# A convolution and a gated unit on one core: row exchanges by transfers in both halves, four more spectrum buffers, closing sums on VectorE, and a rewritten order

## The chip, the core and the metric

The kernel runs on one core of a Trainium2 chip. A core has TensorE (PE in the profile; its weight loads are PEld), VectorE (DVE), ScalarE (ACT), GpSimd (POOL) and SyncE (SP, which here does nothing but issue transfers, one after another). The time is the device time of the program in microseconds (us). The number to be changed is the median of three runs.

## The reference

With `xn` the layer norm of `u` (2048 tokens, 512 channels), the output is the sum of three things:

```python
x = A_u
xn = _layernorm(x, axis=-1)
return x + _A_ref(xn, ...) + _B_ref(xn, B_w_gate, B_w_up, B_w_down)

# _A_ref: a state space convolution, by FFT of length 2L, plus a skip
K = jnp.einsum("dn,dnl,dn->dl", Cc, P, dB).real      # kernel of each channel, P = exp(dt*A*l)
y = irfft(rfft(u) * rfft(K))[:, :L] + u * Dskip

# _B_ref: a gated linear unit, 512 -> 1792 -> 512
h = _sigmoid(x @ w_gate) * (x @ w_up)
return h @ w_down
```

## The kernel before

The gated unit is dense work for TensorE: four groups of 512 tokens (`grp`, L1016), in each 14 blocks of `w_gate` products (L1036) and 14 of `w_up` products (L1060), four matmuls of 512 columns to a block, then four `w_down` products (L1105) of 14 matmuls each. ScalarE takes the sigmoid (L1048), and ScalarE or VectorE takes `up` out of PSUM and multiplies (L1072, L1076).

The convolution is laid between this work. It has these stages:

- The kernel spectra: for four chunks of channels, tables are made on VectorE and ScalarE (L735 to L795) and multiplied on TensorE (L820); each chunk's result goes out to `k_scr` (L831) and comes back (L836). The products of the fourth chunk free the memory of the tables.
- The first transform of `xn`: L694, out to `z_scr` by way of a copy (L287 is the line of the helper that all such copies share).
- Sixteen units (L867 to L935): two halves of the channels (`p` 0 and 1), in each eight groups of frequencies in the order of `UNITS`. A unit loads its part of `z_scr` (L874), makes the spectrum of x on TensorE (L882), copies it to a buffer `xx` (`ex`, L886), exchanges rows between pairs of 32 partitions within `xx`, loads a table `E` (L897), makes the kernel spectrum (L904), multiplies both on VectorE (L909 and L913), turns the product back on TensorE (`mv_`, L926), copies it (`ev`, L930) and stores it to `v_scr` (L933).
- The reload of `v_scr` (`reload`, L963): three parts, the first half's units (part 0), and of the second half the first six units (part 1) and the last two (part 2); each in four pieces. Two of the pieces of part 2 are issued on ScalarE's queue, the others on SyncE's.
- The last transform (L985, L988), added to the unit's output. For token tiles of the first three groups it is `final` (L990): the sum with the gated unit's output, which lies in `glu_sb`. For tiles in `FIN_ACT` (1, 3 and 5 of six) TensorE adds that output by two matmuls with the identity (`fi`, L999) and ScalarE copies the sum (L1007); for the others VectorE adds while it reads PSUM (L1011). The last group's four tiles are summed in L1125. The `w_down` products of the last group are laid between.

The exchange of rows is done in two ways. In the first half (`p == 0`, L890) each unit issues four transfers of 64 KB from SBUF to SBUF on SyncE's queue. In the second half (L893 to L896) VectorE does four copies of 32 partitions.

What sets the order: nothing is scheduled at run time. Every step is an entry of a list (`_Plan.add`, L264), numbered in the order in which the code makes them, and `ORDER` (L202) is a permutation of these numbers written out by hand. Each engine, and each queue of transfers, works its steps strictly in the order in which they stand there; what a step needs of others it waits for with semaphores, and everything behind it on that engine or queue waits too. Buffers that rotate are pools (`_Slot`): `acq` takes the home that has been free longest, `rel` gives it back. The spectrum buffers `xx` have three homes (L856), and a fourth once the tables are free (L846). The buffers of outputs (`ot`) are three.

Of the kernel before, what the change touches and what calls it, by code (L numbers as in the profile page):

```python
# [44 lines left out]
FIN_ACT = (1, 3, 5,)  # L45
# [18 lines left out]
KB = 1024  # L64
# [114 lines left out]
def _consts():  # L179
# [138 lines left out]
def kernel(  # L318
# [74 lines left out]
    OFF = {}  # L393
# [10 lines left out]
    xn = at(OFF["xn"], [NT, D])  # L404
# [457 lines left out]
    def slot(pool, shape):  # L862
        sl = _Slot(pool)
        return sl, lambda: at(HOME[pool][sl.idx], shape)

    v_st = [[] for _ in VPART]
    for p in range(NP):  # L867
        dsl = slice(DW * p, DW * p + DW)
        for u in UNITS[p]:
# [22 lines left out]
            else:  # L892
                def f_sw(xx=xx):  # L893
                    for b in range(4):
                        V.tensor_copy(out=half_of(xx, b, 1), in_=half_of(xx, b ^ 1, 0))  # L895
# [299 lines left out]
```

## Time and profile before

| | |
|---|---|
| runs, median (lowest, highest) | 219.86 us (218.53, 219.88) |
| profiled execution, span on the core | 217.6 us |
| PE busy | 209.0 us, 96% |
| DVE busy | 193.8 us, 89% |
| ACT busy | 179.5 us, 83% |
| DMA, packets of the main queue | 63.8% of 16 engines |

The profile is one execution; its span runs from the first instruction to the last on the core, and it carries no other time of its own. The runs' median lies 2.26 us above that span. Durations and moments in this document that have no other source are those of the profiled execution, counted from the start of its span. Matmuls are pipelined: a row gives 380 ns for one of 512 columns, while a block of four takes 0.86 us.

### The profile page before, as it was taken

How to read it: one execution, taken by the hardware profiler on the slowest of the kernel's cores; microseconds unless marked ns; L12 is line 12 of the kernel's file. 1: busy time of each engine (PE TensorE's matmuls, PEld its weight loads, DVE VectorE, ACT ScalarE, POOL GpSimd, SP SyncE). 2: the span in 40 equal slices, each digit the busy share in tenths (PEclk: the TensorE clock that was granted, in tenths of full speed). 3: DMA queues.
4: the chain of work that ended last, by engine and by line, in shares of the span. 5: the costliest groups of instructions: out<-in, count | busy, mean ns of one | idle time of the engine just before them, and what ended most of it. 6: DMA issues, size and time to landing. Idle time of an engine off the chain costs nothing.

```text
span 217.6 us, 4946 instructions
## 1 busy us (share of the span) xinstructions
PE 209.0 (96%) x1876; PEld 104.0 (48%) x1876; DVE 193.8 (89%) x438; ACT 179.5 (83%) x286; POOL 18.8 (9%) x40
## 2 busy tenths in 40 slices
PE   7979999999999999989999999999999999999894
PEld 2435444444444454435455565445546556544463
DVE  3989999999999999999999999999999999970433
ACT  3799999999999999869989999976897999960111
POOL 1410202002100020012000002010800000000000
PEclk9999999999999999999999999999999999999999
DMA  6999936001463689865697679929959969984974
GB/s 186 316 369 390 299 116 146 0 3 48 145 156 97 233 249 156 264 143 105 166 271 202 183 224 209 239 79 216 216 116 252 282 188 263 267 245 139 269 256 166
DMA packets 51530, 42.80 MB, mean 197 GB/s; under 512 B 16434, under 2 KB 43571, under 8 KB 51507
## 3 DMA queue, kind: packets, MB, share of 16 engines
q1 hardware_dynamic: 50338, 40.60, 63.8%
q0 software_dynamic: 864, 1.57, 5.5%
q10 hardware_dynamic: 304, 0.33, 0.6%
q8 instruction: 14, 0.23, 0.4%
q14 instruction: 10, 0.07, 0.1%
HBM read 25.97 MB, written 12.85 MB: 178 GB/s over the span
## 4 chain that ended last, share of the span: by engine, by line
PE 64%; DMA 17%; ACT 8%; SPq 7%; issue 2%; DVE 0%; ACTq 0%
PE bank L1060 18%; PE bank L1036 16%; PE bank L1105 10%; PE pair L904 7%; SPq L421 7%; DMA wu_sb<-in_B_w_up_dram 5%; PE pair L926 4%; ACT big L287 4%; DMA z_scr<-big 3%; DMA big<-big 3%; DMA big<-z_scr 2%; DMA v_scr<-big 2%; PE pair L882 2%; PE pair L820 2%; ACT us_sb L1072 2%
## 5 line engine op out<-in xcount | busy, mean ns | idle before, releaser
L287 ACT ACTIVATE big<-pair 128x1024 bf16<-128x1024 f32 x64 | 66.2, 1060 | 4.9 <-PE pair L926 1.5
L1060 PE MATMUL bank<-xnT,wu_sb 128*128 128x512 bf16 x224 | 54.5, 380 | 0.5 <-DMA wu_sb<-in_B_w_up_dram 0.4
L1036 PE MATMUL bank<-xnT,wg_sb 128*128 128x512 bf16 (+1 forms) x220 | 50.7, 368 | 1.9 <-DMA wg_sb<-in_B_w_gate_dram 1.8
L1105 PE MATMUL bank<-wd_sb,hT_sb 128*128 128x512 bf16 (+1 forms) x238 | 50.4, 367 | 0.0
L1036 PEld LDWEIGHTS <-wg_sb 128*128 128x128 bf16 x236 | 22.2, 98 | 26.9 <-issue 2.5
L1105 PEld LDWEIGHTS <-hT_sb 128*128 128x128 bf16 x238 | 22.6, 98 | 25.2 <-issue 1.9
L1060 PEld LDWEIGHTS <-wu_sb 128*128 128x128 bf16 x224 | 20.6, 98 | 25.2 <-issue 3.0
L1048 ACT ACTIVATE hT_sb<-bank 128x512 bf16<-128x512 f32 x52 | 30.9, 636 | 1.2 <-PE bank L1036 1.1
L735 DVE TENSOR_TENSOR big<-big 128x1024 bf16<-128x1024 bf16 (+4 forms) x40 | 26.8, 670 | 0.3 <-ACT big L287 0.2
L736 DVE TENSOR_TENSOR big<-big 128x1024 bf16<-128x1024 bf16 (+4 forms) x40 | 26.7, 667 | 0.0
L1072 ACT ACTIVATE us_sb<-bank 128x512 bf16<-128x512 f32 x40 | 25.9, 648 | 0.3
L909 DVE TENSOR_TENSOR big<-big 128x2048 bf16<-128x2048 bf16 x16 | 19.5, 1218 | 0.6 <-PE pair L926 0.3
L904 PE MATMUL pair<-big 128*128 128x256 bf16 x160 | 19.8, 273 | 0.0
L789 ACT ACTIVATE sq_sb<-big 128x256 bf16<-128x256 bf16 (+2 forms) x20 | 13.8, 691 | 5.1 <-DVE big L741 4.9
L904 PEld LDWEIGHTS <-big 128*128 128x128 bf16 x160 | 15.4, 98 | 4.9 <-issue 1.0
L1076 DVE TENSOR_TENSOR hT_sb<-hT_sb,us_sb 128x512 bf16<-128x512 bf16 x40 | 16.5, 418 | 0.4 <-ACT us_sb L1072 0.3
L740 DVE TENSOR_TENSOR big<-big 128x512 bf16<-128x512 bf16 (+4 forms) x40 | 16.5, 414 | 0.1
L741 DVE TENSOR_TENSOR big<-big 128x512 bf16<-128x512 bf16 (+4 forms) x40 | 16.5, 413 | 0.0
L1007 ACT ACTIVATE big<-pair 128x1024 bf16<-128x1024 f32 x3 | 3.1, 1023 | 15.2 <-PE pair L985 12.4
L895 DVE COPY big<-big 32x1024 bf16<-32x1024 bf16 x32 | 13.4, 419 | 0.6
L1011 DVE TENSOR_TENSOR big<-pair,glu_sb 128x1024 bf16<-128x1024 f32 x2 | 2.5, 1226 | 11.7 <-PE pair L985 8.1
L541 DVE BATCH_NORM_STATS2 stats<-big 128x6 f32<-128x512 bf16 x15 | 9.8, 682 | 3.4 <-DMA big<-in_A_u_dram 3.4
(104 smaller groups left out, 244.3 us busy)
## 6 DMA issues: line engine op xcount, KB each, us to landing
big<-c_E SPq DMA_DIRECT2D x16, 320.0 KB, 3.9
z_scr<-big SPq DMA_DIRECT2D x16, 256.0 KB, 2.9
big<-z_scr SPq DMA_DIRECT2D x16, 256.0 KB, 4.9
v_scr<-big SPq DMA_DIRECT2D x16, 256.0 KB, 3.1
big<-in_A_u_dram SPq DMA_DIRECT2D x4, 512.0 KB, 8.2
big<-big SPq DMA_DIRECT2D x32, 64.0 KB, 3.6
wu_sb<-in_B_w_up_dram SPq DMA_DIRECT2D x2, 896.0 KB, 10.7
wd_sb<-in_B_w_down_dram SPq DMA_DIRECT2D x1, 1792.0 KB, 15.1
```

What stands on the lines that cost most here:

```text
L287: nc.scalar.activation(out=get(out), in_=get(in_), func=ACT.Identity)
L735: V.tensor_tensor(out=wide(outp), in0=wide(lo), in1=mre, op=ALU.mult)
L736: V.tensor_tensor(out=wide(tb()), in0=wide(lo), in1=mim, op=ALU.mult)
L740: V.tensor_tensor(out=outp[:, :, 0], in0=outp[:, :, 0], in1=tb()[:, :, 1], op=opr)
L741: V.tensor_tensor(out=outp[:, :, 1], in0=outp[:, :, 1], in1=tb()[:, :, 0], op=opi)
L904: T.matmul(two(sk)[:, o:o + DW], es()[:, g, kt, :], kTv[p][:, :, kt, :], start=kt in (0, NKT - 1), stop=kt >= NKT - 2)
L909: V.tensor_tensor(out=pp().rearrange("p q h m -> p (q h) m"), in0=xx().rearrange("p q h m -> p (q h) m"), in1=kb()[:, 0:2 * DW].unsqueeze( ...
L1036: T.matmul(bank(sl, k % 2)[:, c0:c1], w[:, kt, k * 128:(k + 1) * 128], xnT[:, grp, kt, c0:c1], start=(kt == 0), stop=(kt == KT - 1))
L1048: S.activation(out=hT_sb[:, hs.idx, k % 2, :], in_=bank(sl), func=ACT.Sigmoid)
L1060: T.matmul(bank(sl), wu_sb[:, kt, k * 128:(k + 1) * 128], xnT[:, grp, kt, :], start=(kt == 0), stop=(kt == KT - 1))
L1072: S.activation(out=us_sb[:, us.idx, :], in_=bank(sl), func=ACT.Identity)
L1105: T.matmul(bank(po)[:, 0:c[1] - c[0]], hT_sb[:, hts[k // 2].idx, k % 2, jj * 128:(jj + 1) * 128], wd_sb[:, k, c[0]:c[1]], start=first and ...
```

## The change

- The exchange of rows is done by four transfers in the second half as well; the VectorE copies of L893 to L896 are gone.
- `xx` gets four more homes (4 KB of each partition each), in the memory that the tables free and that the reload of the second half later fills. So that reload (parts 1 and 2) now also waits for the last use of these buffers, the products of all units of the second half (`x_done`).
- `FIN_ACT` is empty: all six sums of `final` are done on VectorE, without identity matmuls.
- `ORDER` is written anew: 987 entries in place of 966 (24 transfers more, three steps `fi` fewer).

In the new order, what bears on the end: on TensorE all gate and up blocks and all units' `mv_` stand ahead of the first two `w_down` products of the last group, and behind the last `mv_` come one small product (L955), then these two; before, one up block, one filler matmul (L521) and one identity pair stood there as well. On SyncE, the load of `x` for the last group moves ahead of the fourth chunk's read-back; between that read-back and the last transfer of the last unit's exchange stand 43 issues, the last included (26 of them exchanges); then seven more up to the last unit's store, among them pieces 3 and 1 of part 0. All pieces of part 1 are issued behind that store, and piece 2 of part 0 after two of the outputs. On SyncE early on, the load of `w_down` moves behind the first layer-norm transfers.

```diff
-FIN_ACT = (1, 3, 5,)
+FIN_ACT = ()
...
-    0, 1, 2, 14, 28, 38, ... 961, 964, 965]
+    0, 1, 2, 14, 28, 38, ... 896, 985, 986]
...
-    kgen[3][0].rel += tuple(_Slot(k, i) for k, i in (("xx", 3), ("vs", 2), ...))
+    kgen[3][0].rel += tuple(_Slot(k, i) for k, i in (("xx", 3), ("xx", 4), ("xx", 5), ("xx", 6), ("xx", 7), ("vs", 2), ...))
...
-    HOME = dict(xx=[OFF["xn"], OFF["xn"] + US, OFF["xn"] + 2 * US, OFF["lad"] + 12 * KB], ...
+    HOME = dict(xx=[OFF["xn"], OFF["xn"] + US, OFF["xn"] + 2 * US, OFF["lad"] + 12 * KB] + [OFF["tmp"] - 16 * KB + US * k for k in range(4)], ...
...
-    v_st = [[] for _ in VPART]
+    v_st, x_done = [[] for _ in VPART], []
...
-            if p == 0:
-                sws = [dma("SP", lambda xx=xx, b=b: half_of(xx, b, 1), lambda xx=xx, b=b: half_of(xx, b ^ 1, 0), deps=[ex], prio=QP,
-                           pkt=2048, hv=0.5)(64 * KB) for b in range(4)]
-            else:
-                def f_sw(xx=xx):
-                    for b in range(4):
-                        V.tensor_copy(out=half_of(xx, b, 1), in_=half_of(xx, b ^ 1, 0))
-                sws = [pl.add("DVE", 1.5, f_sw, [ex], QP)]
+            sws = [dma("SP", lambda xx=xx, b=b: half_of(xx, b, 1), lambda xx=xx, b=b: half_of(xx, b ^ 1, 0), deps=[ex], prio=QP,
+                       pkt=2048, hv=0.5)(64 * KB) for b in range(4)]
...
             pb_ = pl.add("DVE", 0.62, fpb, [pa_], PKD, acq=[qsl], rel=[ksl, xsl])
+            if p:
+                x_done.append(pb_)
...
-                free = x_use[k] + ([o_pre] if k == 0 else []) if p == 0 and k < 3 else table_free
+                free = x_use[k] + ([o_pre] if k == 0 else []) if p == 0 and k < 3 else table_free if p == 0 else table_free + x_done
```

More of the change, by code (lines that the diff above doesn't have):

```diff
@@ L845 @@
     table_free = [x for c in kgen for x in kgen[c]]
-    kgen[3][0].rel += tuple(_Slot(k, i) for k, i in (("xx", 3), ("vs", 2), ("zx", 2), ("zx", 3), ("zx", 7), ("zx", 8), ("zx", 9)))
+    kgen[3][0].rel += tuple(_Slot(k, i) for k, i in (("xx", 3), ("xx", 4), ("xx", 5), ("xx", 6), ("xx", 7), ("vs", 2), ("zx", 2), ("zx", 3), ("zx", 7), ("zx", 8), ("zx", 9)))
     kgen[2][0].rel += (_Slot("zx", 5), _Slot("zx", 6))
@@ L854 @@
     US = 4 * KB
-    HOME = dict(xx=[OFF["xn"], OFF["xn"] + US, OFF["xn"] + 2 * US, OFF["lad"] + 12 * KB], pp=[OFF["xn"] + 3 * US, OFF["kx"]],
+    HOME = dict(xx=[OFF["xn"], OFF["xn"] + US, OFF["xn"] + 2 * US, OFF["lad"] + 12 * KB] + [OFF["tmp"] - 16 * KB + US * k for k in range(4)], pp=[OFF["xn"] + 3 * US, OFF["kx"]],
                 es=[OFF["W0"], OFF["W0"] + 2560, OFF["W0"] + 5120], kb=[OFF["W0"] + 7680, OFF["W0"] + 9728],
```

86 rows, old and new, of the table ORDER are left out of this document.

## The prediction

> **What bounds the kernel now.** I read the page's totals first, then the waits, the chain of work that ended last, and the timelines of SP, PE and DVE.
>
> ```profile
> span 217.6 us, 4946 instructions
> PE 209.0 (96%) x1876; PEld 104.0 (48%) x1876; DVE 193.8 (89%) x438; ACT 179.5 (83%) x286; POOL 18.8 (9%) x40
> ```
>
> ```profile
> 100.00:140.00 40.00, 40.00 (x519) 21.32 (x517) 39.72 (x93) 38.17 (x68) 1.59 (x5) 1.00 0.81 211
> 157.20:188.00 30.80, 30.80 (x294) 16.61 (x293) 29.60 (x60) 28.39 (x38) 0.62 (x2) 1.00 0.81 223
> ```
>
> The second fence is two stretches: length, busy us of PE, PEld, DVE, ACT and POOL, then granted clock, DMA share and GB/s. PE is full in both and its clock is whole, so nothing that merely frees DVE (29.60 of 30.80 us) gains time unless PE waits for DVE. PE's waits:
>
> ```profile
> POOL big L769 <- PE pair L820: 56.6, 3, 28.8
> ...
> PEld L1060 <- DMA wu_sb<-in_B_w_up_dram: 0.9, 1, 0.9
> ...
> PE pair L882 <- DMA big<-z_scr: 0.7, 1, 0.7
> ```
>
> ```profile
> 201.17 0.30 PE L985 MATMUL pair<-xnT,big 128*64 128x256 bf16 x2
> 202.30 0.30 PE L985 MATMUL pair<-big 128*64 128x256 bf16 x2 [0.83 <-DMA big<-v_scr]
> ```
>
> PE's waits are single and short: 0.9 us (0.4 by PE's own row) for the up weights near 21 us, 0.7 us for `z_scr` near 97 us, and 0.83 us in the tail, for the reload of the last units. The chain shows that tail, and the fourth chunk's products (L820), where the second half sets in:
>
> ```profile
> 154.78 1.41 PE pair L820 x117
> ...
> 192.39 0.80 PE pair L926 x16
> 193.26 1.03 ACT big L287
> 194.31 4.82 DMA v_scr<-big
> 199.21 3.05 DMA big<-v_scr
> 202.30 0.52 PE pair L985 x6
> ...
> 207.48 0.43 PE pair L999 x2
> ...
> 214.51 0.42 DVE big L1125
> ```
>
> From the last unit's L926 on, its store and reload decide: 192.39 to 202.30. L1105 covers most of it.
>
> **The change part by part.** Rows for the parts removed and added (busy us, mean ns):
>
> ```profile
> L1060 PE MATMUL bank<-xnT,wu_sb 128*128 128x512 bf16 x224 | 54.5, 380 | 0.5 <-DMA wu_sb<-in_B_w_up_dram 0.4
> ...
> L909 DVE TENSOR_TENSOR big<-big 128x2048 bf16<-128x2048 bf16 x16 | 19.5, 1218 | 0.6 <-PE pair L926 0.3 <-ACT big L287 0.2
> ...
> L895 DVE COPY big<-big 32x1024 bf16<-32x1024 bf16 x32 | 13.4, 419 | 0.6
> ...
> L913 DVE TENSOR_TENSOR big<-big 128x1024 bf16<-128x1024 bf16 x16 | 10.9, 682 | 0.0
> ...
> L1007 ACT ACTIVATE big<-pair 128x1024 bf16<-128x1024 f32 x3 | 3.1, 1023 | 15.2 <-PE pair L985 12.4 <-DMA out_dram<-big 2.8
> ```
>
> 1. *Copies off DVE.* 32 x 0.419 = 13.4 us of DVE go. No row shows PE waiting for L895, so this alone is worth 0; what hides it is PE's own work. Without that cover it would be worth at most the 13.4 us.
>
> 2. *Exchanges on SP.* 32 issues come in. What an issue costs the queue, and how it is held:
>
> ```profile
> 120.30 0.51 SPq L421 DMA_DIRECT2D big<-big  x1
> ...
> 134.57 0.48 SPq L421 DMA_DIRECT2D big<-z_scr  x1
> ```
>
> ```profile
> 140.48 1.16 SPq L421 DMA_DIRECT2D big<-big  x2
> ...
> 145.93 0.51 SPq L421 DMA_DIRECT2D big<-big  x1
> ...
> 148.41 0.59 SPq L421 DMA_DIRECT2D k_scr<-kq_sb  x1
> ...
> 152.22 0.45 SPq L421 DMA_DIRECT2D big<-z_scr  x1
> ```
>
> ```profile
> 157.16 1.26 SPq L421 DMA_DIRECT2D k_scr<-kq_sb  x2
> ...
> 161.56 0.36 SPq L421 DMA_DIRECT2D big<-k_scr  x1
> 161.97 0.58 SPq L421 DMA_DIRECT2D c_scr<-k_scr  x1
> ```
>
> ```profile
> v_scr<-big SPq DMA_DIRECT2D x16, 256.0 KB, 3.1
> ...
> big<-big SPq DMA_DIRECT2D x32, 64.0 KB, 3.6
> ...
> wd_sb<-in_B_w_down_dram SPq DMA_DIRECT2D x1, 1792.0 KB, 15.1
> ...
> xnT<-v_scr SPq DMA_DIRECT2D x3, 512.0 KB, 5.6
> ```
>
> From 148.41 to 152.22 stand six issues: 0.635 us each, nothing awaited. From 120.30 to 134.57 stand 21: 0.68 each, small waits included. An exchange lands 3.6 us after its issue (median); the fastest that the chain shows took 2.40:
>
> ```profile
> 141.06 2.40 DMA big<-big
> ```
>
> In the changed order SP has 43 issues between the fourth chunk's read-back and the last exchange of the last unit, that one included; before, 27 took it to the last store but one. So I lay two paths from the fourth L820 to the last unit's L926, and the later one holds.
>
> - *Where they start.* One filler matmul more stands ahead (0.2); the up blocks that waited 0.4 to 0.9 stand later, and the `z_scr` wait has a block more of PE work ahead of it: -0.6 and -0.7. Against that, the `w_down` load goes behind the first layer-norm transfers. Its price isn't shown; it took 15.1 us in a crowd and was not awaited. Bounds 0 and 1 us; I take 0.2, since the queue it now meets is emptier. Start 154.78 + 0.2 - 1.3 + 0.2 = 153.9.
> - *PE's path.* 192.39 - 154.78 = 37.6 before; one up block more (L1060: four at a pitch of 0.216, 0.86 us): 192.4.
> - *SP's path.* First `k_scr` store 157.16 - 154.78 = 2.4 after the start, 156.3; read-back 4.4 later (161.56 - 157.16, a wait for that store), 160.7; next issue +0.4; the 43rd 42 x 0.635 = 26.7 on, 187.8; lands +3.6, 191.4; L909 and L913, 1.22 + 0.68, 193.3.
>
> SP's path is later by 0.9 us: PE waits there. Bounds: 0 (exchanges landing in 2.4) to +1.9 more at a pitch of 0.68 (43 x 0.045).
>
> [...]
>
> 3. *New homes, and the reload's wait (x_done).* The homes let L882 run ahead: 0 on PE, which is full anyway. The wait puts part 1 of the reload behind the last products; in the new order its pieces are issued behind the last store in any case: 0 beyond that. What it delays is counted next.
>
> 4. *The trip after the last L926.* Start of L926 to end of its copy: 193.26 + 1.03 - 192.39 = 1.9, so 195.2. The store then stood behind a 384 KB piece and took 4.82; now none of part 1 is ahead, but pieces 1 and 3 of part 0 are. Between 3.1 (median) and 4.82 I take 3.5, nearer the median since those two leave some 5 us earlier: 198.7. Reload 3.05: 201.8. Part 1's 768 KB share that time; at 223 GB/s they take 3.5 us, so they just fit. PE reaches this point 201.17 - 192.39 = 8.8 after L926 before; one up block (0.86), a filler (0.2) and one identity pair (0.43) have gone from there: 193.3 + 7.3 = 200.6. It waits 1.2 us, in place of 0.83.
>
> 5. *Closing sums.* Three identity pairs go, 3 x 0.43 = 1.29 us of PE; three copies of 1.02 go from ACT; DVE gets three sums. One pair was cover (4), two are in the tail: -0.86 on PE. But now DVE ends last:
>
> ```profile
> 204.06 1.28 DVE L1125 TENSOR_TENSOR big<-bank,big 128x512 bf16<-128x512 f32 x2
> ...
> 212.41 1.21 DVE L1011 TENSOR_TENSOR big<-pair,big 128x1024 bf16<-128x1024 f32 x1
> 214.51 0.42 DVE L1125 TENSOR_TENSOR big<-bank,big 128x256 bf16<-128x256 f32 x1 [0.89 <-PE bank L1105]
> ```
>
> Before, L1011 for the fifth tile began 212.41 - 202.30 = 10.1 after the reload; now 9.25, then 1.21 + 1.21 + 0.42 = 12.1, against 214.93 - 202.30 = 12.6. So -0.5. Piece 2 of part 0 (512 KB) is now issued behind two outputs, which wait for DVE's first three sums (before, they ended at 204.06 + 1.28, 3.0 after the reload): some 3.6 after it. At the 5.6 us of its kind (`xnT<-v_scr`) it lands 9.2 after. The tile that needs it has its sum at 9.25 and its product 0.8 before that. Bounds 0 and 1.5 us (two outputs' 256 KB ahead of it); I take 0.3.
>
> *Sum.* 201.8 + (217.6 - 202.30) - 0.5 + 0.3 = 216.9, that is 0.7 us under the profiled span. The runs' median lies 2.26 over that span; I keep this: 219.86 - 0.7 = 219.2 us.
>
> **The rivals.**
>
> - *PE stays the only bound* (faster). Nothing on SP is late, the reload and the late piece are covered: 216.9 - 0.9 - 1.2 - 0.3 = 214.5, in runs 216.8. For it: the first half already lives with these transfers, and PE is full there (40.00 of 40.00). Against: there the eight units had longer and SP had idle time; now 43 issues fill its stretch.
> - *SP's queue becomes the bound* (slower). One mechanism: SP issues in order, so a copy that ends late (`ex` or `ev`) holds all that follows, and the last exchange leaves later by as much. For it: the two exchanges from 140.48 on took 1.16 us, and the next left at 145.93: 4.3 us without an issue, since ACT's copy for it came late. SP then had slack to make up; now it has none. Price: pitch 0.68 (+1.9) and half such a hold (+2.1): 216.9 + 4.0 = 220.9, in runs 223.2. It decides slower by over 1% when the 43rd issue leaves 2.9 us or more after 187.8. Against: ACT has no more work than before, and most copies stand well ahead of their transfers. [...]
> - *The tail's transfers crowd.* The late piece costs its whole 1.5 us: 218.1, in runs 220.4.
>
> **How the numbers follow.** About 1% is what a measurement of this kernel can tell from no change: its runs span 218.53 to 219.88. The likeliest case, 219.2, has 0.42 (its own range: 218.0 to 220.5, by the bounds of the landing times); crowding 0.10; PE alone 0.20; SP as the bound 0.28. Within 1% (217.7 to 222.1): 0.42 + 0.10 = 0.52; faster 0.20; slower 0.28. Leaving out 0.07 of "PE alone" and 0.13 of "SP as the bound", the range is 216.6 to 223.4.
>
> **What would show it.** Step 1: no L895, DVE some 10 us less busy (13.4 less three sums of 1.2), PE's busy stretch no shorter for it. Step 2: SP issuing back to back from 160 to 188 with a pitch near 0.64, and PE idle 0.5 to 1.5 us ahead of the last L926, released by DVE L913. Steps 3 and 4: the first L985 waits about 1.2 us, for part 2 or part 1 of the reload. Step 5: DVE ends last, 12 us after that. The forecast is wrong if SP shows long holds while PE waits for L926 at several units, if PE never waits there, or if `w_down` makes the first L1105 wait by over 1 us.

## The result and the profile after

The changed kernel takes 229.85 us (median of four runs, 227.98 to 231.02) against 219.56 for the kernel before (four runs as well): a ratio of 1.049, with a 95% interval of 1.042 to 1.056. It is slower, outside the forecast's range. (A run over 1.5% above the fastest of its kernel counts as disturbed; ratios leave such runs out, so they are not always the quotient of two medians, and the profiles of experiments 3, 9 and 13 are of such runs.) Intervals stand in brackets. The profiled execution has a span of 227.7 us, 10.1 more than before and 10.8 more than the 216.9 forecast. In `after`, lines up to the exchange are numbered as before; behind it L904 is L898, L909 L903, L926 L922, L985 L981, L1036 L1032, L1060 L1056, L1105 L1101.

The totals of the page of the changed kernel, and its instruction queue (packets, MB, share):

```profile
span 227.7 us, 4931 instructions
PE 207.9 (91%) x1844; PEld 104.5 (46%) x1870; DVE 184.1 (81%) x409; ACT 176.0 (77%) x283; POOL 18.4 (8%) x40
...
q8 instruction: 14, 0.23, 0.4%
```

PE is busy for 91% of the span and not 96%. The stretches show where (length, busy us of PE, PEld, DVE, ACT, POOL, then granted clock, DMA share, GB/s); first the changed kernel, then the kernel before over the same two stages, from the fourth L820 to the read-back of `k_scr` and on to the last `mv_`, cut to whole us; the two short stretches between are of the changed kernel:

```profile
155.00:172.00 17.00, 12.14 (x215) 6.22 (x217) 6.08 (x10) 10.95 (x15) 1.39 (x3) 1.00 0.89 210
172.00:201.00 29.00, 28.68 (x263) 15.52 (x265) 19.05 (x31) 23.51 (x30) 0.00 (x0) 0.94 0.76 205
...
172.00:175.00 3.00, 3.00 (x14) 1.84 (x13) 1.61 (x3) 1.78 (x2) 0.00 (x0) 0.50 0.61 161
...
212.80:216.20 3.40, 3.07 (x20) 1.91 (x18) 3.03 (x4) 0.00 (x0) 0.00 (x0) 0.50 0.80 221
```

```profile
154.00:165.00 11.00, 10.87 (x204) 5.14 (x203) 10.74 (x23) 9.79 (x15) 3.53 (x2) 1.00 0.73 172
165.00:193.00 28.00, 28.00 (x276) 15.69 (x274) 27.03 (x51) 24.68 (x31) 0.18 (x1) 1.00 0.88 253
```

Between 155 and 172 us PE stands still for almost 5 of 17 us while the DMA share is 0.89, where it had been 0.73. After that PE is full again, but for 3.4 us, twice, at half its clock. PE's timeline names the places:

```profile
113.03 1.25 PE L898 MATMUL pair<-big 128*128 128x256 bf16 x10 [1.64 <-DVE big L841]
...
155.51 1.38 PE L820 MATMUL pair<-big 128*32 128x82 bf16 x124
159.58 0.22 PE L820 MATMUL pair<-big 128*32 128x82 bf16 x4 [2.69 <-issue]
...
170.76 1.52 PE L898 MATMUL pair<-big 128*128 128x256 bf16 x11 [1.96 <-DMA big<-big]
...
200.39 0.84 PE L922 MATMUL pair<-big 64*64 64x512 bf16 x16
...
211.57 0.30 PE L981 MATMUL pair<-big 128*64 128x256 bf16 x2 [3.64 <-DMA big<-v_scr]
```

VectorE's row for the same read-back, and then the two rows of the kernel before that show how well it fitted there:

```profile
170.38 0.28 DVE L841 TENSOR_TENSOR big<-big,dskr 1x256 bf16<-1x256 bf16 x1 [3.39 <-DMA big<-k_scr]
```

```profile
165.24 0.28 DVE L841 TENSOR_TENSOR big<-big,dskr 1x256 bf16<-1x256 bf16 x1
```

```profile
165.69 2.35 PE L904 MATMUL pair<-big 128*128 128x256 bf16 x20
```

Four waits: two ahead of the first L898 of a half (the read-back of `k_scr`; the fourth row names an exchange, but L841, which adds to the read-back and waited for it, ended at 170.66, just before L898 began), one inside L820 for nothing that the profile shows, one for the reload. What the forecast looked for, a wait ahead of the last L922, isn't there: that L922 is the row at 200.39. Each of the two half clocks takes 3.4 / 2 = 1.7 us of PE's work away, an estimate from the two short stretches.

### The profile page after: what moved, and what is told of

Same layout as the page of the kernel before. It is cut to its first block, busy times and chain, and to the rows that moved or that the text cites. A ratio compares the mean times of both kernels' runs of the same rounds, so it can differ in the third digit from the quotient of the medians.

```text
span 227.7 us, 4931 instructions
## 1 busy us (share of the span) xinstructions
PE 207.9 (91%) x1844; PEld 104.5 (46%) x1870; DVE 184.1 (81%) x409; ACT 176.0 (77%) x283; POOL 18.4 (8%) x40
## 4 chain that ended last, share of the span: by engine, by line
PE 30%; ACT 27%; DMA 15%; DVE 14%; issue 10%; SPq 1%; POOL 0%; DVEq 0%; ACTq 0%; POOLq 0%
ACT big L287 9%; PE bank L1101 8%; PE pair L898 6%; PE bank L1056 5%; PE bank L1032 5%; DMA v_scr<-big 5%; ACT hT_sb L1044 4%; ACT us_sb L1068 4%; DVE stats L541 3%; ACT big L662 3%; DMA out_dram<-big 3%; DMA big<-k_scr 3%; PE pair L922 3%; ACT big L668 2%; DVE big L609 2%
## 5 line engine op out<-in xcount | busy, mean ns | idle before, releaser
L287 ACT ACTIVATE big<-pair 128x1024 bf16<-128x1024 f32 x64 | 66.9, 1074 | 12.3 <-PE pair L898 7.6
L1056 PE MATMUL bank<-xnT,wu_sb 128*128 128x512 bf16 x214 | 53.6, 379 | 1.1 <-ACT us_sb L1068 0.4
L1032 PE MATMUL bank<-xnT,wg_sb 128*128 128x512 bf16 (+1 forms) x211 | 50.9, 371 | 2.3 <-DMA wg_sb<-in_B_w_gate_dram 1.6
L1101 PE MATMUL bank<-wd_sb,hT_sb 128*128 128x512 bf16 (+1 forms) x231 | 50.8, 368 | 0.8 <-issue 0.5
L1032 PEld LDWEIGHTS <-wg_sb 128*128 128x128 bf16 x236 | 22.3, 99 | 27.5 <-issue 2.8
L1101 PEld LDWEIGHTS <-hT_sb 128*128 128x128 bf16 x238 | 22.5, 98 | 25.7 <-issue 3.2
L1044 ACT ACTIVATE hT_sb<-bank 128x512 bf16<-128x512 f32 x52 | 31.6, 651 | 1.9 <-PE bank L1032 1.7
L1056 PEld LDWEIGHTS <-wu_sb 128*128 128x128 bf16 x224 | 20.9, 98 | 24.8 <-issue 3.0
L1068 ACT ACTIVATE us_sb<-bank 128x512 bf16<-128x512 f32 x40 | 26.6, 675 | 1.0 <-PE bank L1056 1.0
L903 DVE TENSOR_TENSOR big<-big 128x2048 bf16<-128x2048 bf16 x16 | 19.4, 1221 | 9.7 <-ACT us_sb L1068 3.9
L898 PE MATMUL pair<-big 128*128 128x256 bf16 x160 | 21.0, 282 | 3.6 <-DMA big<-big 2.0
L1072 DVE TENSOR_TENSOR hT_sb<-hT_sb,us_sb 128x512 bf16<-128x512 bf16 x40 | 16.3, 421 | 6.4 <-ACT us_sb L1068 3.6
L898 PEld LDWEIGHTS <-big 128*128 128x128 bf16 x160 | 15.9, 101 | 9.5 <-DMA big<-big 2.4
L1007 DVE TENSOR_TENSOR big<-pair,glu_sb 128x1024 bf16<-128x1024 f32 x4 | 4.9, 1222 | 12.9 <-issue 10.8
L287 ACT ACTIVATE big<-big 128x256 bf16<-128x256 bf16 x30 | 13.7, 514 | 0.0
L922 PE MATMUL pair<-big 64*64 64x512 bf16 (+1 forms) x256 | 13.4, 327 | 0.0
## 6 DMA issues: line engine op xcount, KB each, us to landing
wu_sb<-in_B_w_up_dram SPq DMA_DIRECT2D x2, 896.0 KB, 10.7
```

What stands on the lines that cost most here:

```text
L287: nc.scalar.activation(out=get(out), in_=get(in_), func=ACT.Identity)
L898: T.matmul(two(sk)[:, o:o + DW], es()[:, g, kt, :], kTv[p][:, :, kt, :], start=kt in (0, NKT - 1), stop=kt >= NKT - 2)
L903: V.tensor_tensor(out=pp().rearrange("p q h m -> p (q h) m"), in0=xx().rearrange("p q h m -> p (q h) m"), in1=kb()[:, 0:2 * DW].unsqueeze( ...
L922: T.matmul(two(sv)[o:o + 64, DW * (2 * g + y):2 * DW * (g + 1)], mab[b:b + 64, 2 * u + g, q, :], pq()[b:b + 64, q, ch] if y else pp()[b:b ...
L1032: T.matmul(bank(sl, k % 2)[:, c0:c1], w[:, kt, k * 128:(k + 1) * 128], xnT[:, grp, kt, c0:c1], start=(kt == 0), stop=(kt == KT - 1))
L1044: S.activation(out=hT_sb[:, hs.idx, k % 2, :], in_=bank(sl), func=ACT.Sigmoid)
```

## The experiments

The table has every run: its time, its ratio to the kernel before on the same chip, and four lengths from its profiled execution: from the start of the fourth L820 to L841 (the read-back is there), on to the start of the last `mv_`, on to the first closing product that has the reload, on to the end of the span. The time of the kernel before is the median of its 64 runs beside the experiments; "none" stands where the record gives no ratio.

| | us (median) | ratio [95%] | trip | units | reload | end |
|---|---|---|---|---|---|---|
| before | 218.65 | | 10.8 | 27.1 | 10.0 | 15.3 |
| changed | 229.85 | 1.049 [1.042, 1.056] | 14.9 | 30.0 | 11.2 | 16.1 |
| 1 | 230.97 | 1.047 [1.041, 1.054] | 14.6 | 30.8 | 10.4 | 16.9 |
| 2 | 232.43 | 1.059 [1.052, 1.067] | 15.2 | 31.5 | 11.7 | 17.3 |
| 3 | 238.3 | none | 15.7 | 32.6 | 11.6 | 17.3 |
| 4 | 231.1 | 1.055 [1.050, 1.060] | 14.4 | 31.2 | 10.8 | 15.9 |
| 5 | 237.07 | 1.082 [1.074, 1.091] | 11.4 | 40.3 | 12.6 | 15.3 |
| 6 | 229.1 | none | 11.9 | 32.5 | 10.4 | 16.3 |
| 7 | 231.27 | 1.057 [1.051, 1.063] | 14.3 | 29.8 | 12.0 | 17.2 |
| 8 | 219.48 | 1.0045 [1.0015, 1.0075] | 10.7 | 27.1 | 9.1 | 16.5 |
| 9 | 227.89 | 1.032 [1.021, 1.042] | 14.4 | 30.2 | 9.7 | 17.4 |
| 10 | 219.3 | 1.002 [0.999, 1.006] | 11.0 | 27.0 | 10.0 | 15.8 |
| 11 | 230.46 | 1.054 [1.052, 1.057] | 13.9 | 32.8 | 10.5 | 16.8 |
| 12 | 228.68 | 1.047 [1.040, 1.054] | 12.0 | 30.4 | 11.4 | 16.3 |
| 13 | 223.31 | 1.022 [1.016, 1.028] | 10.7 | 28.4 | 9.8 | 16.9 |
| 14 | 228.61 | 1.052 [1.044, 1.059] | 11.2 | 31.4 | 11.0 | 17.1 |
| 15 | 217.86 | 0.999 [0.995, 1.002] | 10.7 | 26.3 | 9.9 | 15.0 |
| 16 | 224.82 | 1.027 [1.021, 1.033] | 10.5 | 27.6 | 11.9 | 15.6 |
| 17 | 227.77 | 1.039 [1.032, 1.045] | 12.0 | 30.5 | 11.8 | 16.8 |
| 18 | 222.11 | 1.018 [1.011, 1.025] | 11.0 | 27.0 | 10.0 | 16.2 |

My first theory was that four fixed waits of the new order and the half clocks behind two of them are the loss. Its rival was that the transfers on SyncE are. Experiments 9, 10, 13, 16 and 18 leave a part of the computation out; they price it and are no versions of the kernel.

### The waits one by one: experiments 1 to 4

**1.** The fillers at the start cut differently:

```diff
-            for _ in range(n):
-                T.matmul(bank(wsl), glu_sb[:, 0, 0:128], glu_sb[:, 0, :], start=True, stop=True)
+            for w in (512,) * (n if n < 14 else 10) + (64,) * (20 if n == 14 else 0):
+                T.matmul(bank(wsl)[:, 0:w], glu_sb[:, 0, 0:128], glu_sb[:, 0, 0:w], start=True, stop=True)
```

> The changed kernel, with the filler matmuls at the very start cut differently: 20 of 64 columns in place of 4 of 512, so that TensorE's instruction stream is 32 instructions longer ahead of everything else and no other step moves. Theory A (instructions arrive late): PE stood still for 2.7 us inside the fourth chunk's L820, waiting for nothing that the profile shows, while a 16 KB packet of an instruction queue ran; a block boundary of the stream fell on the start of these 256 fast instructions. Shifted by 32, the stall goes: 2.7 us less, about 227.2 us. Rival B (the products wait for a buffer, a table or a crowded transfer): the stall stays, 229.9 us.

PE's timeline of this run:

```profile
155.26 1.47 PE L820 MATMUL pair<-big 128*32 128x82 bf16 x128
...
164.61 0.41 PE L882 MATMUL pair<-big,m 64*64 64x512 bf16 x4 [1.69 <-DMA big<-z_scr]
...
170.27 2.08 PE L898 MATMUL pair<-big 128*128 128x256 bf16 x9 [2.77 <-DMA big<-big]
```

and SP's:

```profile
157.87 2.64 SPq L421 DMA_DIRECT2D k_scr<-kq_sb  x2
160.61 1.91 SPq L421 DMA_DIRECT2D big<-in_A_u_dram  x1
...
165.75 0.36 SPq L421 DMA_DIRECT2D big<-k_scr  x1
```

Theory A was right on the stall, which is gone, and wrong on the time: the `k_scr` stores left 2.8 us sooner, but the read-back that waits for them left at 165.75 instead of 164.92. It was issued 7.9 us after the first store, when both stores had landed; in the kernel before it was 4.4. The trip stays at 14.6 us, and PE waits at L882 and L898 instead.

**2.** The first L898 of each half behind two more blocks (numbers are entries of `ORDER`; 478 and 613 are the products, 479 and 614 their copies, 829, 849, 962, 919 blocks of the gated unit):

```diff
-    ... 829, 479, 849, 403, 459, 790, 853, ... 453, 613, 903, 523, 962, 614, 561, 439, 919, ...
+    ... 829, 849, 790, 853, 478, 479, 403, 459, ... 453, 903, 962, 439, 919, 963, 918, 613, 523, 614, 561, ...
```

> The changed kernel, with the first kernel-spectrum products of each half (L898) behind two more blocks of the gated unit on TensorE (1.73 us later in its order), their copies behind those blocks' copies on ScalarE; nothing else. Theory A: the trip of the kernel products through k_scr takes some 12.5 us, the new order leaves 10 to 10.8 us of TensorE work for it, so PE waits 1.8 us at 111 and 2.1 us at 169, and the second wait sets the granted clock to a half for 3.4 us (1.7 us more). All three go: 5.6 us less, about 224.3 us. Rival B (exchanges are late anyway): the waits move to L903 and L922 of the same units, and less than 2 us is won, 228 us or more.

No gain: neither theory. The waits ahead of the first L898 of each half went (the next L898 waits 1.1 and 0.7 us, for ScalarE), but the stall in L820 was 3.6 us here, with 6.8 us of half clock behind it, and the wait for the reload grew from 3.6 to 4.2.

**3.** Pieces 3 and 1 of part 0 (870, 868) issued behind piece 0 (867):

```diff
-    ... 867, 554, ... 604, 870, 572, ... 573, 868, 540, ...
+    ... 867, 870, 868, 554, ... 604, 572, ... 573, 540, ...
```

> The changed kernel, with pieces 3 and 1 of part 0 of the reload (1 MB) issued right behind piece 0 on SyncE's queue, some 14 us earlier, ahead of the last 20 exchanges and stores; nothing else. Theory A: in the last 12 us before the closing products some 3 MB of stores and reloads are more than the DMA engines carry (busy share 0.89 to 1.0), so the last units' reload lands 5.2 us after its issue in place of 3.05. Without this 1 MB the wait falls from 3.8 to 1.5 us or less and the half clock behind it goes: 3 to 4 us less, about 226 us. Rival B: part 1's own 768 KB, issued when the last of its stores lands, are what crowds: within 0.5 us of 229.9. Rival C: the 1.2 us more on SP ahead of the exchanges make PE wait for L922: slower than 229.9.

The slowest of all. PE waited 1.2 and 1.8 us for two L922, as rival C says; but the run had lost 3.8 us on the changed kernel by the fourth L820 already, ahead of anything that was moved, so I draw nothing from its time. Theory A isn't borne out in its profile: the last store went 2.5 us ahead of its reload and no longer 3.5, but the reload then took 7.0 us and PE waited 4.0 for it. Experiment 18 repeats the edit where SyncE has no exchanges.

**4.** The new order with VectorE copies:

```diff
-            sws = [dma("SP", ...)(64 * KB) for b in range(4)]
+            if p == 0:
+                sws = [dma("SP", ...)(64 * KB) for b in range(4)]
+            else:
+                sws = [pl.add("DVE", 1.5, f_sw, [ex], QP)]
```

> The changed kernel and its order, but the second half's exchanges on VectorE again (four copies of 32 partitions for each unit, at the place of the unit's last transfer in the order); 24 steps fewer. Theory A (the order's spacing, the late instructions and the tail's transfers cost the time, not the exchanges themselves): PE's stall in the fourth L820 stays at 2.7 us and the wait at 111 us at 1.8; the read-back of the second half lands about 1 us sooner and the tail is less crowded: 226 to 229 us. Rival B (SP's queue with 32 exchanges is what costs): the time falls back to 219 to 221 us. Rival C (VectorE is now the bound, 13.4 us more on it): 230 us or more, PE waiting for L903 and L907.

231.1, with the stall in L820 at 3.6 us: as slow as with transfers. Rival B fell: taking the second half's transfers off SyncE gives nothing back, in this order. The time is rival C's, and VectorE is busy for 29.4 of 31 us from 171.5 on, but PE waits for its products at one L927 (this kernel's `mv_`) alone, for 1.2 us; experiment 14 returns to this.

### Order and transfers apart: experiments 5, 9 and 10

**5.** The order of before, with transfers (each `sws` entry becomes four, the code as in the changed kernel, but `xx` keeps the four homes of before where the changed kernel has eight).

```diff
-            else:
-                sws = [pl.add("DVE", 1.5, f_sw, [ex], QP)]
+            sws = [dma("SP", ...)(64 * KB) for b in range(4)]
```

> The kernel before, in its own order, with the second half's exchanges as four transfers on SyncE in place of the VectorE copies (990 entries: the four stand where the one copy stood); no new spectrum homes, FIN_ACT as before. Theory A (the new order's spacing costs the time, transfers as such next to nothing): within 2 us of the kernel before, 217 to 221 us. Rival B (32 more issues and their traffic cost what was lost): 224 us or more, with PE waiting for L909 or L926 of the second half.

Rival B, and far beyond it: 18 us slower. Its waits between 165 and 182 us (us in total, times, longest):

```profile
DVE big L903 <- DMA big<-big: 9.6, 1, 9.6
...
PE pair L920 <- ACT big L287: 7.6, 1, 7.6
```

VectorE waits 9.6 us for one unit's exchange, and behind it PE stands for 7.6 us (L920 is this kernel's `mv_`). SP had issued back to back from 160.61 on when this unit's four transfers left, from 169.75 to 171.60; they landed by 175.7. This is the prediction's second rival, SP's queue as the bound, though by a full queue and not by a copy that holds it. What the missing homes add is not taken apart.

**9 and 10.** No exchange in the second half, in the new order and in that of before:

```diff
-            sws = [dma("SP", ...)(64 * KB) for b in range(4)]
+            if p == 0:
+                sws = [dma("SP", ...)(64 * KB) for b in range(4)]
+            else:
+                sws = [ex]
```

> The changed kernel with the second half's exchanges left out altogether (32 transfers gone, no VectorE copies in their place: the products read whatever stands in the unexchanged half; 955 entries), everything else in the new order. It prices the transfers against the order. Theory A (the second half's transfers, of which 13 are issued between 145 and 168 us, crowd the fourth chunk's trip through k_scr and the stores; the order adds its own part): 223 to 227 us. Rival B (the order's spacing alone costs the 10 us): 229 us or more, as with VectorE copies. Rival C (the transfers are all of it): 220 us or less.

> The kernel before with the second half's 32 VectorE copies left out, nothing in their place (the products read whatever stands in the unexchanged half; 958 entries). It prices step 1 of the prediction. Theory A (13.4 us of copies on VectorE are worth nothing while PE is full): within 0.7 us of the kernel before. Rival B (VectorE is a second bound in that stretch): 1.5 us or more faster.

Without any exchange in the second half the changed kernel is still slower by 3.2% [2.1, 4.2], some 7 us; the transfers add 1.7%, some 4 us. (The ratio of 9 rests on two runs.) In the order of before, leaving out 13.4 us of VectorE copies gains nothing, the ratio being 1.002 [0.999, 1.006]: step 1 of the prediction holds. So the larger part of the loss is not the transfers'. It is the rest of the change, the order above all (the closing sums alone are 1.0 us, experiment 8); yet in this order, and with eight homes, transfers are bearable (229.85 where the old order with four has 237).

### The fourth chunk's trip: experiments 6 and 11

**6.** Experiment 1, with the load of x (967) and a GpSimd transfer (706) moved out of the trip:

```diff
-    ... 371, 436, 967, 951, ... 529, 563, ... 540, 706, 541, 589, 375, ...
+    ... 371, 436, 951, ... 529, 967, 563, ... 540, 541, 589, 375, 706, ...
```

> The changed kernel with the filler matmuls cut differently as in the first experiment, and two transfers taken out of the fourth chunk's trip through k_scr: the 512 KB load of x for the last group goes behind the store of the second half's second unit on SyncE (some 25 us later), and one 256 KB accumulating transfer on GpSimd (into glu_sb) goes behind the last small GpSimd copy (some 15 us later). Theory A (the trip is long because its stores land late in a crowd: 6.3 us in the first experiment, where SP issued the read-back 8 us after the first store and not 4.4): the read-back leaves 2 to 3 us sooner, the wait ahead of the second half's first L898 (2.9 us) falls under 1 us and the half clock behind it goes: 3 to 4.5 us less than the first experiment's 231, 226.5 to 228. Rival B (the trip is bound by SP's queue or by its own small packets): no gain, 230 us or more.

The trip falls from 14.6 to 11.9 us, since the stores land in 4.5 us and not in 7.3, which is Theory A's mechanism. PE still waits 1.8 us at L898, not under 1, and the time hardly follows (229.1, runs from 226.43 to 230.76): in their place the next unit's exchange, landing late, makes VectorE wait 7.1 us and PE 2.7.

**11.** Experiments 4 and 1 together.

```diff
-            for _ in range(n):
+            for w in (512,) * (n if n < 14 else 10) + (64,) * (20 if n == 14 else 0):
...
-            sws = [dma("SP", ...)(64 * KB) for b in range(4)]
+                sws = [pl.add("DVE", 1.5, f_sw, [ex], QP)]
```

> The new order with VectorE copies in the second half (as in the fourth experiment) and the filler matmuls cut differently (as in the first): is the order alone slow because its instruction stream stalls in the fourth L820? Theory A: the 3.8 us stall goes, the read-back of the second half ends some 3 us sooner, since no second-half transfer is in its way, and the time is 2 to 3 us less than the fourth experiment's 231: 228 to 229. Rival B (as with the transfers, the wait only moves to the read-back): 231.

Rival B: the stall goes, the trip is still 13.9 us with no second-half transfer in it, and its stores need over 7 us to land. So the crowd is the order's: exchanges of the first half, stores, the load of x. Of these only the load of x was taken out by itself, with one GpSimd transfer, in 6.

### Limits on top of each other: experiments 12, 13 and 14

**12.** Experiments 6 and 2, and one up block (944) behind the last `mv_` (542):

```diff
-    ... 935, 944, 573, ... 961, 542, 624, ...
+    ... 935, 573, ... 961, 542, 944, 624, ...
```

> The changed kernel with four edits together: fillers cut differently, the x load and the GpSimd transfer out of the fourth chunk's trip, the first kernel-spectrum products of each half 1.73 us later on TensorE, and one up block moved behind the last L926 as cover for the last reload. Theory A (waits at fixed places add up, and each over about 2 us costs a further 1.7 us at half clock): against the 229.1 of the kernel with the first two edits, 1.0 + 2.0 + 1.7 for the two read-back waits and 0.9 for the cover: 223.5 to 226 us. Rival B (exchanges that land late take the place of the waits: L903 waited 7.1 us for one in that kernel): 228 us or more.

**13.** The same without exchanges and without the moved block (the edit of experiment 9).

```diff
-    ... 542, 944, 624, ...
+    ... 542, 624, ...
...
+                sws = [ex]
```

> The new order with the second half's exchanges left out (as in the ninth experiment, the products read what stands there), the fillers cut differently, the x load and the GpSimd transfer out of the fourth chunk's trip, and the first kernel-spectrum products 1.73 us later: the twelfth kernel without its exchanges and without its cover block. It tells whether the transfers take the place of the waits that the edits remove. Theory A (several limits lie on top of each other: the trip through k_scr and the exchanges' landing; with both gone the middle of the kernel is as fast as before, and only the tail's wait is left): 220.5 to 224 us, the last L922 near 195 us. Rival B (the new order is slow in the middle for a reason of its own that none of the edits touches): 226 us or more.

The stretches of 12 from the fourth L820 on, then of 13:

```profile
156.00:168.00 12.00, 12.00 (x213) 5.76 (x212) 5.67 (x8) 10.98 (x16) 0.18 (x1) 1.00 0.77 184
168.00:200.00 32.00, 27.48 (x269) 15.42 (x267) 18.88 (x31) 23.16 (x30) 1.04 (x2) 1.00 0.84 225
```

```profile
158.00:169.00 11.00, 11.00 (x208) 5.25 (x207) 5.55 (x9) 10.28 (x15) 0.24 (x1) 1.00 0.75 182
169.00:198.00 29.00, 28.30 (x275) 15.91 (x273) 19.32 (x32) 23.82 (x31) 1.04 (x2) 1.00 0.75 206
```

In both the first stretch is full: the fixed waits there are gone, and 0.7 us at L898 is left in the second. There PE idles 4.5 of 32 us with the transfers and 0.7 of 29 without (1.5 of 27.5 in experiment 16, which keeps these edits). Theory A of 13 holds, and rival B of 12: once the waits are gone, the exchanges that had been late behind them show, at 2.5% between the two (5.4 us; the block moved in 12 is in that difference). In 12 VectorE waits 9.9 us for two units' exchanges. One limit had hidden the other, as far as runs on two chips can tell.

**14.** The kernel of 13, with VectorE copies.

```diff
-                sws = [ex]
+                sws = [pl.add("DVE", 1.5, f_sw, [ex], QP)]
```

> The same kernel as the one without exchanges, but with the VectorE copies of the kernel before in their place: a whole computation in the new order. Theory A (VectorE has room for them: it was busy 15 of 25 us in the unit stretch of the changed kernel): within 1.5 us of the kernel without exchanges. Rival B (the new order leaves the products no time for copies ahead of them, so that PE waits for L907): 3 us or more above it.

Its stretch of the units:

```profile
167.00:199.00 32.00, 28.33 (x273) 15.66 (x272) 30.17 (x58) 23.31 (x30) 1.14 (x2) 1.00 0.67 188
```

Rival B. VectorE is busy for 30.2 of 32 us and PE for 28.3: in this order VectorE, with 1.8 us of idle time left, is the likely bound when it copies; PE's rows name it for 1.5 us of waits, ScalarE's copies for 2.1. The room that I had read off the changed kernel (19 of 29 us) was idle time at the wrong moments.

### The tail: experiments 7, 16, 17 and 18

**7.** The reload split after five units, and two pieces of part 1 (874, 871) ahead of the last store (544):

```diff
-    VPART = ((0, 0, 8, 4), (1, 0, 6, 4), (1, 6, 8, 4))
+    VPART = ((0, 0, 8, 4), (1, 0, 5, 4), (1, 5, 8, 4))
...
-    ... 946, 968, 544, 874, 871, 875, ...
+    ... 946, 968, 874, 871, 544, 875, ...
```

> The changed kernel with the second half's reload split after five units and not after six, and the two pieces of part 1 that the tail needs first issued ahead of the last unit's store. Theory A (the tail's wait of 3.8 us is there because all of part 1 waits for the sixth unit's store, which the new order puts 3.8 us ahead of the last store where it had been 5.6, so that 1.5 MB of part 1 stand between the last store and its reload): the wait falls to 1 to 2 us and the half clock after it (1.7 us) goes: 3 to 4 us less, about 226 us. Rival B (the tail is bound by the last store's own trip, landing and reload): unchanged wait, 229 to 231 us.

Nearest to rival B in its time, but the waits for the reload grew to 5.2 us, which neither theory has. The pieces left 2.6 us sooner, but the last store behind them was followed by its reload only 5.5 us later, where it had been 3.5.

**16 and 17.** Both last blocks behind the last `mv_`, without exchanges (16, from 13) and with them (17, from 12):

```diff
-    ... 534, 942, 956, ... 935, 944, 573, ... 961, 542, 624, ...
+    ... 534, 956, ... 935, 573, ... 961, 542, 942, 944, 624, ...
```

> The new order without the second half's exchanges and with the three edits of the thirteenth kernel, and beside these the last gate and the last up block (1.73 us) moved behind the last L922 on TensorE, their ScalarE work behind that L922's copy. It prices the tail. Theory A (the tail's wait of 2.4 us is there because the new order leaves 6.6 us of work under the last units' trip where 8.3 stood before): the wait falls to about 0.7 us and no half clock follows it: 2.5 to 3.5 us less than the thirteenth kernel's 223.3, near 220. Rival B (the trip itself is what got longer, or the last L922 can't start sooner): 222.5 us or more.

> The twelfth kernel, with the transfers, with the gate block too behind the last L922 (two blocks of cover in place of one) and their ScalarE work behind that L922's copy. Theory A (cover is what the tail lacks): the wait falls from 2.9 to about 2 us and with it, if the half clock stays away, 1.7 us more: 226 us. Rival B (the exchanges of the last unit land too late for its L922 to start sooner): within 1 us of 228.7.

Rival B in both. Work under the trip doesn't help, because the way from the last `mv_` to the reload stretches: 11.9 us in 16 and 9.8 in 13, with 2.4 and 2.2 us of wait. No half clock followed in 16, and it isn't faster for it.

**18.** Experiment 16 with the edit of experiment 3.

```diff
-    ... 867, 554, ... 604, 870, 572, ... 573, 868, 540, ...
+    ... 867, 870, 868, 554, ... 604, 572, ... 573, 540, ...
```

> The sixteenth kernel (new order, no second-half exchanges, middle mended, two blocks of cover) with pieces 3 and 1 of part 0 of the reload, 1 MB, issued right behind piece 0, some 14 us earlier, when SyncE has no exchanges to issue. Theory A (this 1 MB shares the DMA engines with the last stores and part 1, so that the last store takes 3.9 us and its reload 5.75): both fall towards the 3 to 4 us of the kernel before, the tail's wait goes from 2.6 to 1 us or less: 222 to 223.5 us. Rival B (part 1's own pieces, all behind the last store, are what crowds): the wait stays above 2 us, 224 us or more.

The reload of the last two units had been slower from the start. Its groups of transfers (count, KB each, median us to landing) around the last store, in the kernel before and in the changed one:

```profile
v_scr<-big SPq DMA_DIRECT2D x2, 256.0 KB, 3.7
...
big<-v_scr SPq DMA_DIRECT2D x2, 128.0 KB, 3.5
```

```profile
v_scr<-big SPq DMA_DIRECT2D x2, 256.0 KB, 4.6
big<-v_scr SPq DMA_DIRECT2D x2, 128.0 KB, 7.1
```

The two medians of 128 KB are not of like pieces: in the changed kernel the landing of only the second is known. The first, for which PE waits, went 5.3 us ahead of PE's product where it had landed in 3.05; the second took 7.1 where it had taken 4.0. PE's timeline of 16, then of 18:

```profile
207.68 0.30 PE L982 MATMUL pair<-big 128*64 128x256 bf16 x2 [2.40 <-DMA big<-v_scr]
```

```profile
204.00 0.30 PE L982 MATMUL pair<-big 128*64 128x256 bf16 x2 [0.44 <-DMA big<-v_scr]
```

Theory A: the way from the last `mv_` falls from 11.9 to 10.0 us and the wait to 0.4 (another of 1.2 follows in the closing products). The median is 2.7 us lower, though the intervals overlap. In a kernel without exchanges, then, most of the tail's wait came from 1 MB of part 0's reload among the last stores. For the changed kernel itself that is not shown: in experiment 3 the same edit left the wait at 4.0 us. 18 is still 1.8% [1.1, 2.5] above the kernel before; 1.5 us of that stand ahead of the fourth L820 in its profile, and I did not take them apart.

### Two edits of the kernel before: experiments 8 and 15

**8.** `FIN_ACT` alone.

```diff
-FIN_ACT = (1, 3, 5,)
+FIN_ACT = ()
```

> The kernel before, in its own order, with FIN_ACT empty: three identity pairs less on TensorE, all six closing sums on VectorE; nothing else. Theory A (step 5 of the prediction: 0.5 us less at the end and 0.43 us less cover): 0.3 to 0.9 us less than the kernel before. Rival B (VectorE's six sums with three output buffers become the end's chain): 1 us or more slower.

1.0 us slower [0.3, 1.6], the sign opposite to step 5 and the size rival B's. Its profiled execution is no longer than that of before (217.1), so it can't show why: there PE ends 2.1 us sooner and the span 0.5, and VectorE waits 1.1 us for output buffers where it had waited 4.9. The cause stays open.

**15.** An up block (933, its copy 934) behind the last `mv_` (533):

```diff
-    ... 558, 933, 914, 894, 946, 533, 905, 934, ... 534, 23, ...
+    ... 558, 914, 894, 946, 533, 933, 905, ... 534, 934, 23, ...
```

> The kernel before with one up block (four matmuls, 0.86 us) moved on TensorE from ahead of the last L926 to behind it, its copy on ScalarE behind the copy of that L926; nothing else. Theory A (the last units' trip through v_scr sets the end, and what stands behind the last L926 is cover for it; the product that L926 needs was ready before): 0.4 to 0.9 us less than the kernel before. Rival B (L926 then waits for VectorE's product instead): no difference, within 0.3 us.

PE's rows show no wait for the reload any more (0.83 us before) and that execution's span is 216.2, as Theory A says, but over twelve runs the time is the same (0.999 [0.995, 1.002]). With the whole computation it is the version nearest to the kernel before; whether it beats it is not shown.

## Why the prediction was wrong

In the prediction's own terms the span was to be 153.9 + 39.4 + 8.5 + 15.1 = 216.9 (start of the fourth L820, to the last `mv_`, to the reload, to the end). It was 155.5 + 44.9 + 11.2 + 16.1 = 227.7.

- *Where they start* (+1.6; +2.0 by PE's timeline, where the fourth L820 of before begins at 154.44 and not at the 154.78 of the chain's row). The waits near 21 and 97 us went, as forecast, and `w_down` cost nothing. But the new order has 10.9 us of PE work between that half's last L820 (100.52) and its first L898, the old one 12.2, and the trip through `k_scr` takes 12: PE waited 1.6. I had costed what left this stretch and not what moved closer together in it.
- *PE's path* (44.9 for 38.5, and 5.5 over the 39.4 of the sum) is the step that failed. I took 37.6 us of the old trace plus one block, that is, PE full. It stood 2.7 us in L820 and 2.0 at L898, and the half clock took 1.7: together the 6.4. The trace of before could have told that the trip just fitted (L841 10.8 us after the start of L820, the first L904 0.5 us later). In the changed kernel the trip takes 14.9 us: the first store leaves 5.2 us after L820's start and not 2.7, which is the stall; the read-back is issued 4.2 us behind it (4.4 before) and takes 5.4 us to land, not 3.7. From 149.7 to 165 us the new order issues nine exchanges where there had been two, and the load of x; I counted them as issues on SP and gave the trip its old landing times. Without the stall the stores land late instead (experiment 1); experiment 6 shows that the load of x and a GpSimd transfer make most of that, and experiments 16 and 18, without the second half's exchanges too, are back at 10.5 and 11.0 us.
- *SP's path* was nearly right from the read-back on: its 43rd issue left 29.5 us after that (27.1 forecast) at a pitch of 0.687, not 0.635, and landed in 2.1 us, not 3.6. But the read-back itself left 9.4 us after the start, not 6.8. The wait of 0.9 did not show, because PE was later than SP: the last L907 ended at 199.9, L922 began at 200.4. With PE's waits removed, PE waited 2.3 and 1.4 us for L922 (experiment 12), though at other units than the last. So the second rival was a real cost, hidden.
- *The trip after the last L926* (+2.7). Cover was 7.2 us (7.3 forecast) and the store took 3.5, as forecast; but from L922 to the end of its copy it took 2.4 us, not 1.9, and the reload 5.3, not 3.05. "They just fit" was the error. That 1 MB of part 0 shared the DMA engines is shown for the kernel without exchanges (experiment 18) and only likely here. It would be the third rival, with other pieces of part 0 than the one that I had priced.
- *Closing sums* (+1.0): alone they cost 1.0 us, not -0.5 (experiment 8). The second half clock falls here too, and how the two share the +1.0 is not shown.
- *Copies off DVE*: worth 0, as forecast (experiment 10). *New homes*: not tried alone. *x_done*: nothing lost; the last product ended at 199.9, and part 1's first piece left at 203.7, behind the last store (202.8).
- Two costs had no term at all: PE's stall inside L820 (2.7 us), and the granted clock of 0.50 behind two of its waits (1.7 us each, by the estimate above). The trace of before has neither.

## What to carry to other kernels

When an order is rewritten, measure the distance on the critical engine between each store and the first use of its read-back, old and new, and price the trip with the transfers that now share it; a trip that just fitted is the first thing to break. Removing the one wait that a profile shows proves little where several limits lie close together: remove the suspected resource itself, on both orders, and compare. And a schedule tuned around one means of moving data is not neutral: transfers in the old order cost 18 us, while in the new order copies gained nothing over transfers.

## What the runs showed of the hardware

- *PE stalls where an instruction packet comes late.* A 16 KB packet of the instruction queue (14 or 15 in each trace) stands near each fourth L820, whose 256 instructions (matmuls and weight loads) take 1.4 to 1.8 us where nothing stalls. In all five runs where it came 1.5 to 2.9 us after L820's start (the changed kernel and experiments 2, 3, 4, 9) PE stalled for 2.7 to 3.8 us ahead of its last three or four matmuls; in the other fifteen profiles it came 1.0 to 3.3 us ahead of L820, and none stalled there by more than 0.4. Shifting the stream by 32 instructions moved the packet from 1.5 us behind the start to 2.9 ahead of it, and the stall went (experiment 1). What makes the packet late is not shown; that a boundary of the stream fell on L820's start was my guess in Theory A of experiment 1, and no run shows it.
- *The clock drops behind a wait.* In these profiles 23 of the 32 waits of 1.9 us or more in PE's rows were followed by 3.4 or 6.8 us at a granted clock of 0.50, which began 2.0 to 5.0 us after PE had stopped; no shorter wait was (the longest is 1.85). Of the 23, 15 were shorter than 3.4 us. So a gap of 2 us can cost 3.7 (an estimate: 2.0 of waiting and the 1.7 above), as the one at 168.8 us in the changed kernel did, and it need not: one of 3.6 us in experiment 4 had no half clock behind it. The spread of 1.3% in the changed kernel's runs isn't explained by it, since their mean granted clocks are all 0.982 to 0.985.
